# K stage in three-slot bundles, with R and convolution in K's PSUM ring: a fused convolution and channel mix on one core

## Chip, cores, metric

One core of one Trainium2 chip. The metric is device time in microseconds (us) of one execution, slowest core; here there is only one. The kernel before takes 466.56 us (median of 4 runs).

## The reference

```python
w = softmax(weight)                            # [8 heads, 7 taps]
y = causal depthwise convolution of x with w   # x: [8, 4160, 192]; 24 channels a head
y_prev = y shifted by one position
xk = mu_k * y + (1 - mu_k) * y_prev
xr = mu_r * y + (1 - mu_r) * y_prev
k = relu(xk @ w_k)                             # 192 -> 1024
v = (k * k) @ w_v                              # 1024 -> 192
out = sigmoid(xr @ w_r) * v
```

## The kernel before

A slot is one K tile: 128 of the 1024 channels of k at 512 positions of two batches (1024 columns), 8 slots a step. The batches are taken in four pairs, here called quarters, of 65 slots each. Channels are 192 = 128 + 64; the 64 rest channels of two batches lie in one tile, so their matmuls use 64-row halves of the array side by side. Two slots make a bundle, ordered so that the 64-row matmuls of both stand together:

```python
psK = tile_pool(bufs=2, PSUM)   # K tiles, two banks each
psV = tile_pool(bufs=2, PSUM)   # V, one bank each
psM = tile_pool(bufs=2, PSUM)   # convolution, transposes, R: one bank each

def k_mm(n):                    # slot n
    ps = psK.tile([P, 2, BANK], FP32, tag="k")
    first = j % 2 == 0
    go(first, True)             # even slot: 128-row matmuls, then 64-row ones; odd: the reverse
    go(not first, False)
# ... cut
at_ = n0 + ns + 2               # slot of a step's first V tile
# ... cut
for ns in bundles():            # per bundle of two slots
    for n in ns: run(early, n)  # loads of x
    for n in real: k_mm(n)
    for n in ns:
        run(act, n)             # ScalarE: convolution out of PSUM, sigmoid
        run(pe, n)              # convolution, transposes, R, V
        k_relu(n)               # ScalarE
        run(dve, n)             # VectorE: difference, mixes, v_out; SP: y_write, y_read
        k_square(n - 1)         # VectorE
```

Convolution gives y with time on partitions; K needs channels there. For the first four groups of blocks TensorE transposes y. From the fifth on y goes through memory: `y_write` stores it to `y_drams`, `y_read` fetches it with a transposing DMA into `yT`. Both are issued from the SP queue, as are all outputs.

Of the kernel before, what the change touches and what calls it, by code (L numbers as in the profile page):

```python
# [14 lines left out]
def kernel(  # L15
# [29 lines left out]
    WARM = 40  # L45
# [5 lines left out]
    psK = ctx.enter_context(tc.tile_pool(name="psK", bufs=2, space=bass.MemoryType.PSUM))  # L51
    psV = ctx.enter_context(tc.tile_pool(name="psV", bufs=2, space=bass.MemoryType.PSUM))
    psM = ctx.enter_context(tc.tile_pool(name="psM", bufs=2, space=bass.MemoryType.PSUM))
# [19 lines left out]
    for p in range(NPAIR):  # L73
        blk0 = 0
        for nb, s, on_pe in (
            ((3, 0, True), (4, 1, True), (4, 2, True), (5, 3, True), (10, 4, False), (6, 6, False), (3, 8, False))
            if p == 0
            else ((10, 0, False), (8, 2, False), (8, 4, False), (9, 6, False))
        ):
            groups.append((p, blk0, nb, steps[first_step[p] + s][3], on_pe))  # L80
            blk0 += nb
# [109 lines left out]
    def conv_mm(g, c, pool=None, tag="m"):  # L191
        nb = groups[g][2]
        if c == 0:
            ys[g] = two.tile([P, GB, 2 * D], BF16, tag="y", name="y")
        hs = chunks(g)[c]
        ps = (pool or psM).tile([P, nb, 2, G * len(hs)], FP32, tag=tag, name="ps_c")
        conv_ps[g, c] = ps
        for i, h in enumerate(hs):
            nc.tensor.matmul(  # L199
                out=ps[:, :, :, i * G : (i + 1) * G],  # L200
                lhsT=toe[:, h, :],
                rhs=xbs[g][:, :nb, :, h * G : (h + 1) * G],
                start=True,
                stop=True,
            )
# [43 lines left out]
    def tr_mm(g, j):  # L249
# [3 lines left out]
        ps = psM.tile([P, 3, 2, BLK], BF16, tag="m", name="ps_t")  # L253
# [21 lines left out]
    def diff(s):  # L275
        p, t0, L, _, _ = steps[s]
        c0 = YC + t0
        d = two.tile([P, 3, STEP], BF16, tag="diff", name="d")
# [48 lines left out]
    def k_mm(n):  # L327


        s, j = slots[n]  # L330
        p, _, L, _, _ = steps[s]
        if L == TAIL:
            return k_mm_tail(n, p)
        xk = xks[s]
        ps = psK.tile([P, 2, BANK], FP32, tag="k", name="ps_k")
        k_ps[n] = ps
        first = j % 2 == 0
        nf = STEP // L


        def go(hi, start):
            for f in range(nf):
                fs = slice((j * nf + f) * P, (j * nf + f + 1) * P)
                for i in range(2):
                    r = slice(0, P) if hi else slice(i * LO, (i + 1) * LO)
                    nc.tensor.matmul(  # L346
                        out=ps[:, i, f * L : (f + 1) * L],
                        lhsT=wk[r, 0 if hi else 1, fs],
                        rhs=xk[r, i if hi else 2, :L],
                        start=start and f == 0,  # L350
                        stop=not start and f == nf - 1,
                    )

        go(first, True)
        go(not first, False)
# [42 lines left out]
    for s, (p, t0, L, n0, ns) in enumerate(steps):  # L398
        for t in range(max(1, 2 * L // P)):
            at_ = n0 + ns + 2  # L400
            tiles.append((s, t, max(at_, tiles[-1][2] + 1) if tiles else at_))
# [3 lines left out]
    def r_mm(m):  # L405
        s, t, _ = tiles[m]
        p, _, L, _, _ = steps[s]
        q = m - t % 2
        if t % 2 == 0:
            r_ps[q] = psM.tile([P, 2, D], FP32, tag="m", name="ps_r")  # L410
        o = r_ps[q][:, t % 2, :]
        if L > TAIL:
            xr = xrs[s]
            st, c = divmod(t * P, L)
            hi, lo, wlo = xr[:, st, c : c + P], xr[:, 2, c : c + P], wr[:, 2 + st, :]
        else:
            hi, lo, wlo = tails[p % 2][:, 1, 1, :], tails[p % 2][:, 1, 0, :], wr[:, 1, :]
        nc.tensor.matmul(out=o, lhsT=hi, rhs=wr[:, 0, :], start=True, stop=False)  # L418
        nc.tensor.matmul(out=o, lhsT=lo, rhs=wlo, start=False, stop=True)  # L419

    def r_sig(m):
        ps = r_ps.pop(m)
        n = 2 if steps[tiles[m][0]][2] > TAIL else 1
        r_sb = four.tile([P, 2, D], BF16, tag="r_sb", name="r_sb")
        r_sbs[m] = r_sb
        nc.scalar.activation(out=r_sb[:, :n, :], in_=ps[:, :n, :], func=AF.Sigmoid)  # L426
# [38 lines left out]
    early, pe, act, dve = ({} for _ in range(4))  # L465
# [3 lines left out]

    for g, (p, blk0, nb, n0, on_pe) in enumerate(groups):  # L470
        if g < 2:
            continue
        nc_ = len(chunks(g))
        late = p == 0 and n0 < 30
        if not on_pe:
            per = 2 if late else 1
            c0 = n0 - 20 if late else n0 - 30
            w0, r0 = c0 + -(-nc_ // per), n0 - (11 if late else 17)
        else:
            per = 1  # L480
            c0 = n0 - 14 if n0 > 12 else 1
            r0 = c0 + nc_
        if g > 3:
            at(early, max(c0 - 14, 6 if g == 4 else 10), x_tile, g, nc.vector)
            at(early, max(c0 - 14, 6 if g == 4 else 10), load_x, g)
        for c in range(nc_):
            at(pe, c0 + c // per, conv_mm, g, c)
            at(act, c0 + c // per + 1, conv_out, g, c, nc.scalar.copy)
        if on_pe:
            for j in range((nb + 1) // 2):  # L490
                at(pe, r0 + j, tr_mm, g, j)
                at(dve, r0 + 1 + j, tr_out, g, j, nc.vector.tensor_copy)
        else:
            at(dve, w0, y_write, g)
            at(dve, r0, y_read, g)
    for s, (p, t0, L, n0, ns) in enumerate(steps):
        if s == 0:
            continue
        late = n0 < 14
        at(dve, n0 - (3 if late else 7), diff, s)  # L500
        for j, (i, part) in enumerate(((0, 0), (0, 1), (1, 0), (1, 1))):
            at(dve, n0 + ((-3, -2, -1, 0)[j] if late else j - 5), mix, s, i, part)
    for m, (s, t, vs) in enumerate(tiles):
        at(pe, vs - 2, r_mm, m)
        if t % 2 == 1 or steps[s][2] == TAIL:
            q = m - t % 2
            at(act, vs - 1, r_sig, q)
            at(dve, vs + 1, v_out, q)
        at(pe, vs, v_mm, m)

    def run(table, n):
        for fn, a in table.get(n, ()):
            fn(*a)

    def prologue():
# [23 lines left out]
        warm = psK.tile([P, BANK], FP32, tag="k", name="warm")  # L539
        for _ in range(WARM):  # L540
            nc.tensor.matmul(out=warm, lhsT=ones_t, rhs=zeros, start=True, stop=True)
# [16 lines left out]
        for c in range(n):  # L558
            conv_mm(0, c, psV if c % 2 else None, "v" if c % 2 else "m")
        for c in range(n):  # L560
            conv_out(0, c, act_ if c % 2 == 0 else dve_, act_)
        for j in range(2):
            tr_mm(0, j)
        for j in range(2):
            tr_out(0, j, dve_)
        n = len(chunks(1))
        for c in range(n):
            conv_mm(1, c, psV if c % 2 else None, "v" if c % 2 else "m")
            conv_out(1, c, act_)
        diff(0)  # L570
        for i in range(2):
            for part in range(2):
                mix(0, i, part)
        for j in range(2):
            tr_mm(1, j)
            tr_out(1, j, dve_)
# [3 lines left out]
    def bundles():  # L580

        n = 0
        while n < tiles[-1][2] + 3:
# [53 lines left out]
```

## Time and profile before

| | before |
|---|---|
| time, median | 466.56 us |
| span of the profiled run | 464.4 us |
| TensorE busy | 445.4 us, 96% |
| VectorE, ScalarE busy | 83%, 80% |
| TensorE waits from 60 to 450 us | none listed |

TensorE sets the time from 44 us on; the prediction shows those lines.

Below, a hole is a stretch in which TensorE starts no matmul.

### The profile page before, as it was taken

Reading aid. Unit: us, or ns where it says so; the run is one execution under the profiler, and the core shown is the slowest. Engines: PE = TensorE matmul, PEld = TensorE weight load, DVE = VectorE, ACT = ScalarE, POOL = GpSimd, SP = SyncE. Lnnn points to the kernel's source line nnn. Section 1 sums busy time; section 2 is a strip of 40 time slices with the busy share of each in tenths; the row PEclk is TensorE's granted clock in tenths of the full one; section 3 lists DMA queues with packets and bytes.
Section 4 is the critical chain, followed back from the end, with each engine's and each line's share of the span. In section 5 each row is a group of like instructions: output and inputs, shape, how many; then the busy total and the mean of one; then the engine's idle time right before and its main releaser. Section 6 shows DMA issues by size and latency. Waiting matters only on the chain.

```text
span 464.4 us, 10001 instructions
## 1 busy us (share of the span) xinstructions
PE 445.4 (96%) x3898; PEld 298.3 (64%) x3960; DVE 387.3 (83%) x748; ACT 371.3 (80%) x544; POOL 49.5 (11%) x71
## 2 busy tenths in 40 slices
PE   8787999999999999999999999999999999999996
PEld 3554666666876666566676666666677666666676
DVE  2887799887998889889798989878898987888873
ACT  2598878978878897888979788887978888777771
POOL 6810511000020050000002041000002000000000
PEclk9799999999999999999999999999999999999999
DMA  5993999683469599755367779938166753821223
GB/s 79 164 185 75 181 196 202 120 192 112 105 136 186 141 154 232 148 145 135 99 150 124 182 120 215 220 82 200 55 150 129 165 133 95 167 69 52 69 69 95
DMA packets 134480, 64.18 MB, mean 138 GB/s; under 512 B 85825, under 2 KB 133985, under 8 KB 134433
## 3 DMA queue, kind: packets, MB, share of 16 engines
q1 hardware_dynamic: 96097, 48.60, 41.9%
q0 software_dynamic: 38336, 14.95, 27.7%
q8 instruction: 31, 0.51, 0.5%
q14 instruction: 16, 0.13, 0.1%
HBM read 29.65 MB, written 37.25 MB: 144 GB/s over the span
## 4 chain that ended last, share of the span: by engine, by line
PE 91%; DMA 2%; DVE 2%; ACT 2%; issue 2%; POOL 0%; DVEq 0%
PE ps_k L346 39%; PE ps_v L436 37%; PE ps_r L418 5%; PE ps_r L419 5%; PE ps_c L199 4%; DMA xb<-in_x_dram 1%; ACT k_sb L375 1%; PE ps_k L363 1%; DMA w_raw<-in_weight_dram 1%; ACT y L219 1%; PE ps_t L257 1%; DMA w_scr<-w_row 1%; DVE k L394 0%; ACT y L222 0%; DVE yT L268 0%
## 5 line engine op out<-in xcount | busy, mean ns | idle before, releaser
L375 ACT ACTIVATE k_sb<-ps_k 128x1024 bf16<-128x1024 f32 x260 | 260.1, 1026 | 36.4 <-PE ps_k L346 31.6
L346 PE MATMUL ps_k<-xk,wk 64*128 64x512 bf16 (+2 forms) x994 | 205.3, 377 | 7.5 <-ACT k_sb L375 0.4
L436 PE MATMUL ps_v<-wv,k 128*128 128x192 bf16 x2048 | 210.8, 246 | 0.0
L436 PEld LDWEIGHTS <-k 128*128 128x128 bf16 x2048 | 175.3, 98 | 31.3 <-issue 1.8
L394 DVE TENSOR_TENSOR k<-k_sb 128x1024 bf16<-128x1024 bf16 x256 | 174.9, 685 | 15.0 <-ACT k_sb L375 14.3
L346 PEld LDWEIGHTS <-wk 64*128 64x128 bf16 (+1 forms) x1056 | 56.3, 96 | 109.1 <-issue 108.0
L449 DVE TENSOR_TENSOR o_sb<-ps_v,r_sb 128x384 f32<-128x384 f32 x132 | 72.4, 549 | 35.7 <-PE ps_v L436 33.8
L426 ACT ACTIVATE r_sb<-ps_r 128x384 bf16<-128x384 f32 x132 | 64.4, 488 | 39.3 <-PE ps_r L419 38.8
L418 PE MATMUL ps_r<-wr,xr 128*128 128x192 bf16 x256 | 62.9, 246 | 0.0
L419 PE MATMUL ps_r<-wr,xr 128*128 128x192 bf16 x256 | 62.9, 246 | 0.0
L219 ACT CAST y<-ps_c 120x384 bf16<-120x384 f32 (+4 forms) x96 | 45.0, 471 | 8.8 <-PE ps_c L199 8.8
L199 PE MATMUL ps_c<-xb,toe 128*128 128x384 bf16 (+6 forms) x152 | 43.5, 321 | 4.1 <-ACT y L222 1.8
L323 DVE TENSOR_TENSOR xr<-xr,yT 128x1024 bf16<-128x1024 bf16 (+1 forms) x66 | 36.2, 549 | 2.3
L323 DVE TENSOR_TENSOR xk<-xk,yT 128x1024 bf16<-128x1024 bf16 (+1 forms) x66 | 36.2, 549 | 2.3
L109 POOL DMA_DIRECT2D xb<-in_x_dram x38 | 33.5, 888 | 31.0 <-issue 17.5
L281 DVE TENSOR_TENSOR d<-yT 128x1536 bf16<-128x1536 bf16 (+2 forms) x37 | 31.8, 859 | 3.6 <-DMA yT<-y_dram 3.5
L320 DVE TENSOR_SCALAR xr<-d,mu 128x1024 bf16<-128x1024 bf16 (+1 forms) x66 | 27.9, 423 | 0.1
L108 POOL DMA_DIRECT2D xb<-in_x_dram x8 | 4.4, 552 | 221.1 <-PE ps_k L346 221.1
L320 DVE TENSOR_SCALAR xk<-d,mu 128x1024 bf16<-128x1024 bf16 (+1 forms) x66 | 26.6, 403 | 0.2
L418 PEld LDWEIGHTS <-xr 128*128 128x128 bf16 x256 | 25.0, 98 | 0.0
L419 PEld LDWEIGHTS <-xr 128*128 128x128 bf16 x256 | 25.0, 98 | 0.0
L222 ACT CAST y<-ps_c 120x384 bf16<-120x384 f32 (+9 forms) x52 | 24.0, 466 | 0.4 <-DVE yT L227 0.2
(48 smaller groups left out, 88.5 us busy)
## 6 DMA issues: line engine op xcount, KB each, us to landing
out_dram<-o_sb SPq DMA_DIRECT2D x128, 192.0 KB, 2.4
xb<-in_x_dram POOLq DMA_DIRECT2D x18, 384.0 KB, 10.4
y_dram<-y SPq DMA_DIRECT2D x6, 720.0 KB, 5.4
y_dram<-y SPq DMA_DIRECT2D x4, 900.0 KB, 6.6
xb<-in_x_dram POOLq DMA_DIRECT2D x6, 432.0 KB, 8.1
y_dram<-y SPq DMA_DIRECT2D x3, 810.0 KB, 10.4
xb<-in_x_dram POOLq DMA_DIRECT2D x2, 480.0 KB, 8.8
xb<-in_x_dram POOLq DMA_DIRECT2D x4, 192.0 KB, 6.1
```

The source lines that it names most:

```text
L199: nc.tensor.matmul(out=ps[:, :, :, i * G : (i + 1) * G], lhsT=toe[:, h, :], rhs=xbs[g][:, :nb, :, h * G : (h + 1) * G], start=True, stop=True,
L219: copy(out=yh[:, :, :, c0 : c0 + n], in_=ps[:BLK, :, :, 0:n])
L320: nc.vector.tensor_scalar(out=o, in0=d[:, sl, :L], scalar1=mu[:, i, part : part + 1], scalar2=None, op0=ALU.mult)
L323: nc.vector.tensor_tensor(out=o, in0=o, in1=yT[:, sl, c0 : c0 + L], op=ALU.add)
L346: nc.tensor.matmul(out=ps[:, i, f * L : (f + 1) * L], lhsT=wk[r, 0 if hi else 1, fs], rhs=xk[r, i if hi else 2, :L], start=start and f == ...
L375: nc.scalar.activation(out=k_sb, in_=ps.rearrange("p a b -> p (a b)"), func=AF.Relu)
L394: nc.vector.tensor_tensor(out=o, in0=i, in1=i, op=ALU.mult)
L418: nc.tensor.matmul(out=o, lhsT=hi, rhs=wr[:, 0, :], start=True, stop=False)
L419: nc.tensor.matmul(out=o, lhsT=lo, rhs=wlo, start=False, stop=True)
L426: nc.scalar.activation(out=r_sb[:, :n, :], in_=ps[:, :n, :], func=AF.Sigmoid)
L436: nc.tensor.matmul(out=o, lhsT=k2[:, f, t * P : (t + 1) * P], rhs=wv[:, f, :], start=(f == 0), stop=(f == NF - 1),)
L449: nc.vector.tensor_tensor(out=o_sb[:, :n, :], in0=v_ps.pop(m)[:, :n, :], in1=r_sbs.pop(m)[:, :n, :], op=ALU.mult)
```

## The change

The intent is fewer changes of the row tiling on TensorE (one stretch of 64-row matmuls for three slots instead of two). Three K tiles take six of the eight PSUM banks that the kernel uses, and V two, so R (four tiles at a time) and convolution (two chunks) move into the K ring (the pool whose buffers are handed out in turn), and the early schedule is written anew. Cut to its core:

```diff
-    psK = ... bufs=2        psV = ... bufs=2        psM = ... bufs=2
+    psK = ... bufs=3        psV = ... bufs=2
-        ((3,0,True),(4,1,True),(4,2,True),(5,3,True),(10,4,False),(6,6,False),(3,8,False))
+        ((3,0,True),(4,1,True),(4,2,True),(5,3,True),(10,4,False),(9,6,False))
+    def k_section(ns):
+        for n in ns[:-1]: k_mm(n, True, True)     # 128 rows
+        for n in ns[:-1]: k_mm(n, False, False)   # 64 rows
+        k_mm(ns[-1], False, True)                 # 64 rows
+        k_mm(ns[-1], True, False)                 # 128 rows
-            at_ = n0 + ns + 2
+            at_ = n0 + ns + 1
-            c0 = n0 - 20 if late else n0 - 30
-            w0, r0 = c0 + -(-nc_ // per), n0 - (11 if late else 17)
+            xs = {28: [7, 9, 11, 13], 44: [19, 22, 25, 28]}[n0] if p == 0 else range(n0 - 34, n0 - 34 + 4 * nx, 4)
+            at(dve, xs[-1] + 1, y_write, g)
+            at(dve, xs[-1] + 5, y_read, g)
+            if ns[0] < NSLOT:
+                k_section(ns)
+                for n in ns: k_relu(n)
             for n in ns:
-                run(act, n)
+                run(xt, n)      # R and convolution, matmuls and ScalarE part
                 run(pe, n)      # V (and the transposes)
```

For the first group through memory this moves `y_write` from slot 12 to 14, `y_read` from 17 to 18, and its first reader from 21 to 22. The load of x for the second quarter moves from slot 21 to 17.

More of the change, by code (lines that the diff above doesn't have):

```diff
@@ L44 @@
     YC = 16
-    WARM = 40
+    WARM = 36
     const = ctx.enter_context(tc.tile_pool(name="const", bufs=1))
@@ L50 @@
     four = ctx.enter_context(tc.tile_pool(name="four", bufs=4))
-    psK = ctx.enter_context(tc.tile_pool(name="psK", bufs=2, space=bass.MemoryType.PSUM))
+    psK = ctx.enter_context(tc.tile_pool(name="psK", bufs=3, space=bass.MemoryType.PSUM))
     psV = ctx.enter_context(tc.tile_pool(name="psV", bufs=2, space=bass.MemoryType.PSUM))
-    psM = ctx.enter_context(tc.tile_pool(name="psM", bufs=2, space=bass.MemoryType.PSUM))
     dram = ctx.enter_context(tc.tile_pool(name="dram", bufs=1, space=bass.MemoryType.DRAM))
@@ L75 @@
         for nb, s, on_pe in (
-            ((3, 0, True), (4, 1, True), (4, 2, True), (5, 3, True), (10, 4, False), (6, 6, False), (3, 8, False))
+            ((3, 0, True), (4, 1, True), (4, 2, True), (5, 3, True), (10, 4, False), (9, 6, False))
             if p == 0
-            else ((10, 0, False), (8, 2, False), (8, 4, False), (9, 6, False))
+            else ((10, 0, False), (10, 2, False), (10, 4, False), (5, 7, False))
         ):
@@ L189, in chunks, with conv_mm @@
         return [range(h, min(H, h + n)) for h in range(0, H, n)]
-    def conv_mm(g, c, pool=None, tag="m"):
+    def conv_mm(g, c):
         nb = groups[g][2]
@@ L194, in conv_mm @@
             ys[g] = two.tile([P, GB, 2 * D], BF16, tag="y", name="y")
-        hs = chunks(g)[c]
-        ps = (pool or psM).tile([P, nb, 2, G * len(hs)], FP32, tag=tag, name="ps_c")
-        conv_ps[g, c] = ps
-        for i, h in enumerate(hs):
-            nc.tensor.matmul(
-                out=ps[:, :, :, i * G : (i + 1) * G],
-                lhsT=toe[:, h, :],
-                rhs=xbs[g][:, :nb, :, h * G : (h + 1) * G],
-                start=True,
-                stop=True,
-            )
+        ps2 = psK.tile([P, 2, BANK], FP32, tag="k", name="ps_c")
+        for k, hs in enumerate(chunks(g)[c : c + 2]):
+            w = G * len(hs)
+            ps = ps2[:, k, 0 : nb * 2 * w].rearrange("p (n s c) -> p n s c", n=nb, s=2)
+            conv_ps[g, c + k] = ps
+            for i, h in enumerate(hs):
+                nc.tensor.matmul(
+                    out=ps[:, :, :, i * G : (i + 1) * G],
+                    lhsT=toe[:, h, :],
+                    rhs=xbs[g][:, :nb, :, h * G : (h + 1) * G],
+                    start=True,
+                    stop=True,
+                )
     def conv_out(g, c, copy, copy_lo=None):
@@ L252, in tr_mm @@
             new_yT(p)
-        ps = psM.tile([P, 3, 2, BLK], BF16, tag="m", name="ps_t")
+        ps = psV.tile([P, 3, 2, BLK], BF16, tag="v", name="ps_t")
         tr_ps[g, j] = ps
@@ L277, in diff @@
         c0 = YC + t0
-        d = two.tile([P, 3, STEP], BF16, tag="diff", name="d")
+        d = three.tile([P, 3, STEP], BF16, tag="diff", name="d")
         diffs[s] = d
@@ L325, with k_mm @@
     k_ps, k_sbs, k2s = {}, {}, {}
-    def k_mm(n):
+    def k_mm(n, hi, start):
         s, j = slots[n]
-        p, _, L, _, _ = steps[s]
-        if L == TAIL:
-            return k_mm_tail(n, p)
+        L = steps[s][2]
         xk = xks[s]
-        ps = psK.tile([P, 2, BANK], FP32, tag="k", name="ps_k")
-        k_ps[n] = ps
-        first = j % 2 == 0
+        if start:
+            k_ps[n] = psK.tile([P, 2, BANK], FP32, tag="k", name="ps_k")
+        ps = k_ps[n]
         nf = STEP // L
-        def go(hi, start):
-            for f in range(nf):
-                fs = slice((j * nf + f) * P, (j * nf + f + 1) * P)
-                for i in range(2):
-                    r = slice(0, P) if hi else slice(i * LO, (i + 1) * LO)
-                    nc.tensor.matmul(
-                        out=ps[:, i, f * L : (f + 1) * L],
-                        lhsT=wk[r, 0 if hi else 1, fs],
-                        rhs=xk[r, i if hi else 2, :L],
-                        start=start and f == 0,
-                        stop=not start and f == nf - 1,
-                    )
-        go(first, True)
-        go(not first, False)
+        for f in range(nf):
+            fs = slice((j * nf + f) * P, (j * nf + f + 1) * P)
+            for i in range(2):
+                r = slice(0, P) if hi else slice(i * LO, (i + 1) * LO)
+                nc.tensor.matmul(
+                    out=ps[:, i, f * L : (f + 1) * L],
+                    lhsT=wk[r, 0 if hi else 1, fs],
+                    rhs=xk[r, i if hi else 2, :L],
+                    start=start and f == 0,
+                    stop=not start and f == nf - 1,
+                )
+    def k_section(ns):
+        s, _ = slots[ns[0]]
+        if steps[s][2] == TAIL:
+            return k_mm_tail(ns[0], steps[s][0])
+        for n in ns[:-1]:
+            k_mm(n, True, True)
+        for n in ns[:-1]:
+            k_mm(n, False, False)
+        k_mm(ns[-1], False, True)
+        k_mm(ns[-1], True, False)
     def k_mm_tail(n, p):
@@ L399, with r_mm @@
         for t in range(max(1, 2 * L // P)):
-            at_ = n0 + ns + 2
+            at_ = n0 + ns + 1
             tiles.append((s, t, max(at_, tiles[-1][2] + 1) if tiles else at_))
     r_ps, r_sbs, v_ps = {}, {}, {}
-    def r_mm(m):
-        s, t, _ = tiles[m]
+    def r_mm(m0):
+        s, _, _ = tiles[m0]
         p, _, L, _, _ = steps[s]
-        q = m - t % 2
-        if t % 2 == 0:
-            r_ps[q] = psM.tile([P, 2, D], FP32, tag="m", name="ps_r")
-        o = r_ps[q][:, t % 2, :]
-        if L > TAIL:
-            xr = xrs[s]
-            st, c = divmod(t * P, L)
-            hi, lo, wlo = xr[:, st, c : c + P], xr[:, 2, c : c + P], wr[:, 2 + st, :]
-        else:
-            hi, lo, wlo = tails[p % 2][:, 1, 1, :], tails[p % 2][:, 1, 0, :], wr[:, 1, :]
-        nc.tensor.matmul(out=o, lhsT=hi, rhs=wr[:, 0, :], start=True, stop=False)
-        nc.tensor.matmul(out=o, lhsT=lo, rhs=wlo, start=False, stop=True)
@@ L421, in r_sig @@
-    def r_sig(m):
-        ps = r_ps.pop(m)
-        n = 2 if steps[tiles[m][0]][2] > TAIL else 1
-        r_sb = four.tile([P, 2, D], BF16, tag="r_sb", name="r_sb")
-        r_sbs[m] = r_sb
-        nc.scalar.activation(out=r_sb[:, :n, :], in_=ps[:, :n, :], func=AF.Sigmoid)
+        ps = psK.tile([P, 2, BANK], FP32, tag="k", name="ps_r")
+        r_ps[m0] = ps
+        for k in range(4 if L > TAIL else 1):
+            t = tiles[m0 + k][1]
+            o = ps[:, k // 2, k % 2 * D : (k % 2 + 1) * D]
+            if L > TAIL:
+                xr = xrs[s]
+                st, c = divmod(t * P, L)
+                hi, lo, wlo = xr[:, st, c : c + P], xr[:, 2, c : c + P], wr[:, 2 + st, :]
+            else:
+                hi, lo, wlo = tails[p % 2][:, 1, 1, :], tails[p % 2][:, 1, 0, :], wr[:, 1, :]
+            nc.tensor.matmul(out=o, lhsT=hi, rhs=wr[:, 0, :], start=True, stop=False)
+            nc.tensor.matmul(out=o, lhsT=lo, rhs=wlo, start=False, stop=True)
@@ new lines, in r_sig @@
+    def r_sig(m0):
+        ps = r_ps.pop(m0)
+        if steps[tiles[m0][0]][2] > TAIL:
+            r_sb = three.tile([P, 2, 2 * D], BF16, tag="r_sb", name="r_sb")
+            nc.scalar.activation(out=r_sb, in_=ps[:, :, 0 : 2 * D], func=AF.Sigmoid)
+            for k in range(2):
+                r_sbs[m0 + 2 * k] = r_sb[:, k, :].rearrange("p (t d) -> p t d", t=2)
+        else:
+            r_sb = two.tile([P, D], BF16, tag="r_tail", name="r_tail")
+            nc.scalar.activation(out=r_sb, in_=ps[:, 0, 0:D], func=AF.Sigmoid)
+            r_sbs[m0] = r_sb.unsqueeze(1)
@@ L462, in v_out, with conv, r, tr @@
                 )
-    early, pe, act, dve = ({} for _ in range(4))
+    early, xt, pe, dve = ({} for _ in range(4))
     def at(table, n, fn, *a):
         table.setdefault(n, []).append((fn, a))
+    def conv(g, c):
+        conv_mm(g, c)
+        for k in range(c, min(c + 2, len(chunks(g)))):
+            conv_out(g, k, nc.scalar.copy)
+    def r(m0):
+        r_mm(m0)
+        r_sig(m0)
+    def tr(g, j):
+        tr_mm(g, j)
+        tr_out(g, j, nc.vector.tensor_copy)
     for g, (p, blk0, nb, n0, on_pe) in enumerate(groups):
-        if g < 2:
+        nx = -(-len(chunks(g)) // 2)
+        ntr = (nb + 1) // 2
+        if g == 0:
@@ L472 @@
             continue
-        nc_ = len(chunks(g))
-        late = p == 0 and n0 < 30
-        if not on_pe:
-            per = 2 if late else 1
-            c0 = n0 - 20 if late else n0 - 30
-            w0, r0 = c0 + -(-nc_ // per), n0 - (11 if late else 17)
-        else:
-            per = 1
-            c0 = n0 - 14 if n0 > 12 else 1
-            r0 = c0 + nc_
+        if g == 1:
+            xs, trs = [], [0] * ntr
+        elif on_pe:
+            xs = [[0, 1], [4, 6]][g - 2]
+            trs = [[2, 3], [7, 8, 9]][g - 2]
+        else:
+            xs = {28: [7, 9, 11, 13], 44: [19, 22, 25, 28]}[n0] if p == 0 else range(n0 - 34, n0 - 34 + 4 * nx, 4)
+            trs = []
+            at(dve, xs[-1] + 1, y_write, g)
+            at(dve, xs[-1] + 5, y_read, g)
@@ L483 @@
         if g > 3:
-            at(early, max(c0 - 14, 6 if g == 4 else 10), x_tile, g, nc.vector)
-            at(early, max(c0 - 14, 6 if g == 4 else 10), load_x, g)
-        for c in range(nc_):
-            at(pe, c0 + c // per, conv_mm, g, c)
-            at(act, c0 + c // per + 1, conv_out, g, c, nc.scalar.copy)
-        if on_pe:
-            for j in range((nb + 1) // 2):
-                at(pe, r0 + j, tr_mm, g, j)
-                at(dve, r0 + 1 + j, tr_out, g, j, nc.vector.tensor_copy)
-        else:
-            at(dve, w0, y_write, g)
-            at(dve, r0, y_read, g)
+            at(early, max(xs[0] - 14, 5 if g == 4 else 9), x_tile, g, nc.vector)
@@ L496 @@
+            at(early, max(xs[0] - 14, 5 if g == 4 else 9), load_x, g)
+        for i, n in enumerate(xs):
+            at(xt, n, conv, g, 2 * i)
+        for j, n in enumerate(trs):
+            at(pe, n, tr, g, j)
     for s, (p, t0, L, n0, ns) in enumerate(steps):
         if s == 0:
-            continue
-        late = n0 < 14
-        at(dve, n0 - (3 if late else 7), diff, s)
-        for j, (i, part) in enumerate(((0, 0), (0, 1), (1, 0), (1, 1))):
-            at(dve, n0 + ((-3, -2, -1, 0)[j] if late else j - 5), mix, s, i, part)
+            when = (None, None, None, 1, 1)
+        elif s == 1:
+            when = (0, 0, 1, 4, 5)
+        elif s == 2:
+            when = (5, 6, 7, 9, 10)
+        elif n0 == 28:
+            when = (22, 24, 25, 27, 28)
+        else:
+            when = (n0 - 8, n0 - 6, n0 - 5, n0 - 3, n0 - 2)
@@ L503 @@
+        if when[0] is not None:
+            at(dve, when[0], diff, s)
+        for n, (i, part) in zip(when[1:], ((0, 0), (0, 1), (1, 0), (1, 1))):
+            if n is not None:
+                at(dve, n, mix, s, i, part)
     for m, (s, t, vs) in enumerate(tiles):
-        at(pe, vs - 2, r_mm, m)
+        if t % 4 == 0:
+            at(xt, 2 if s == 0 else vs - 3, r, m)
         if t % 2 == 1 or steps[s][2] == TAIL:
-            q = m - t % 2
-            at(act, vs - 1, r_sig, q)
-            at(dve, vs + 1, v_out, q)
+            at(dve, vs + 1, v_out, m - t % 2)
@@ L513, in run, with warm @@
             fn(*a)
+    def warm(n):
+        ps = psV.tile([P, BANK], FP32, tag="v", name="warm")
+        for _ in range(n):
+            nc.tensor.matmul(out=ps, lhsT=ones_t, rhs=zeros, start=True, stop=True)
     def prologue():
@@ L537, in prologue @@
         )
-        warm = psK.tile([P, BANK], FP32, tag="k", name="warm")
-        for _ in range(WARM):
-            nc.tensor.matmul(out=warm, lhsT=ones_t, rhs=zeros, start=True, stop=True)
+        warm(WARM)
         softmax()
@@ L557, in prologue @@
         n = len(chunks(0))
-        for c in range(n):
-            conv_mm(0, c, psV if c % 2 else None, "v" if c % 2 else "m")
+        for c in range(0, n, 2):
+            conv_mm(0, c)
         for c in range(n):
             conv_out(0, c, act_ if c % 2 == 0 else dve_, act_)
+        warm(2)
         for j in range(2):
@@ L565, in prologue @@
             tr_out(0, j, dve_)
+        warm(5)
         n = len(chunks(1))
-        for c in range(n):
-            conv_mm(1, c, psV if c % 2 else None, "v" if c % 2 else "m")
-            conv_out(1, c, act_)
+        for c in range(0, n, 2):
+            conv(1, c)
         diff(0)
-        for i in range(2):
-            for part in range(2):
-                mix(0, i, part)
-        for j in range(2):
-            tr_mm(1, j)
-            tr_out(1, j, dve_)
+        for part in range(2):
+            mix(0, 0, part)
+        warm(3)
         x_tile(3, nc.vector)
@@ L582, in bundles @@
         n = 0
+        for p in range(NPAIR):
+            rest = sum(st[4] for st in steps if st[0] == p and st[2] > TAIL)
+            twos = rest % 3 * -1 % 3
+            sizes = [2] * twos + [3] * ((rest - 2 * twos) // 3)
+            for w in sizes if p == 0 else sizes[::-1]:
+                yield range(n, n + w)
+                n += w
+            yield range(n, n + 1)
+            n += 1
         while n < tiles[-1][2] + 3:
-            w = 2 if n < NSLOT and steps[slots[n][0]][2] > TAIL else 1
-            yield range(n, n + w)
-            n += w
+            yield range(n, n + 1)
+            n += 1
     with tc.manual_schedule():
@@ L590 @@
         for n in range(-60, 0):
-            for table in (early, act, pe, dve):
+            for table in (early, xt, pe, dve):
                 assert n not in table, n
@@ L595 @@
                 run(early, n)
-            real = [n for n in ns if n < NSLOT]
-            for n in real:
-                k_mm(n)
+            if ns[0] < NSLOT:
+                k_section(ns)
+                for n in ns:
+                    k_relu(n)
             for n in ns:
-                run(act, n)
+                run(xt, n)
                 run(pe, n)
-                if n in real:
-                    k_relu(n)
                 run(dve, n)
```

## The prediction

> **What bounds the kernel now.** I read the page first: engine totals, then the time slices, then the groups.
>
> ```profile
> span 464.4 us, 10001 instructions
> PE 445.4 (96%) x3898; PEld 298.3 (64%) x3960; DVE 387.3 (83%) x748; ACT 371.3 (80%) x544; POOL 49.5 (11%) x71
> PE   8787999999999999999999999999999999999996
> L375 ACT ACTIVATE k_sb<-ps_k 128x1024 bf16<-128x1024 f32 x260 | 260.1, 1026 | 36.4 <-PE ps_k L346 31.6
> L394 DVE TENSOR_TENSOR k<-k_sb 128x1024 bf16<-128x1024 bf16 x256 | 174.9, 685 | 15.0 <-ACT k_sb L375 14.3
> L426 ACT ACTIVATE r_sb<-ps_r 128x384 bf16<-128x384 f32 x132 | 64.4, 488 | 39.3 <-PE ps_r L419 38.8
> ```
>
> TensorE is busy 96% of the span, and the only slices below 9 are the first four and the last. So there are two stages: a start of some 44 us with holes, and a steady stage without any. A table by windows agrees (window, length, then busy time of PE, PEld, DVE, ACT, POOL):
>
> ```profile
> 18.10:43.70 25.60, 21.47 (x166) 12.20 (x168) 20.60 (x39) 21.22 (x35) 6.60 (x9) 0.94 0.99 125
> 43.70:251.00 207.30, 204.04 (x1815) 137.95 (x1843) 182.02 (x353) 175.57 (x259) 21.61 (x28) 1.00 0.78 153
> 251.00:460.20 209.20, 205.61 (x1847) 140.64 (x1875) 177.17 (x335) 168.78 (x240) 9.57 (x12) 1.00 0.59 128
> ```
>
> In the steady stage VectorE is at 86%, ScalarE at 83%; both follow TensorE. The waits of TensorE from 60 to 450 us, listed alone, are empty. So only TensorE issue time, or the start, can make this kernel shorter. "Busy" hides one loss though, seen in the timeline of a bundle without convolution (start, length, engine, line):
>
> ```profile
> 447.25 1.67 PE L346 MATMUL ps_k<-xk,wk 128*128 128x512 bf16 x8
> 448.76 0.82 PE L436 MATMUL ps_v<-wv,k 128*128 128x192 bf16 x8
> 449.42 0.25 PE L418 MATMUL ps_r<-wr,xr 128*128 128x192 bf16 x1
> ...
> 448.21 1.94 ACT L375 ACTIVATE k_sb<-ps_k 128x1024 bf16<-128x1024 f32 x2 [0.27 <-PE ps_k L346]
> ```
>
> The K section of two slots runs from 447.25 to 448.76: 1.51 us. Its eight matmuls are four over 128 rows and two pairs of 64-row ones; the trace's start times show the two of a pair 3 to 4 ns apart. So six streams of 512 columns, 0.216 us each by the trace's starts inside a stretch, are 1.30 us. The remaining 0.21 us is the change of row tiling: start to start from the last 128-row matmul to the first 64-row one is 0.312 us, back again 0.308, and two neighbours lose 0.01 each. There are 128 such bundles: 128 x 0.206 = 26.4 us.
>
> **What the Trainium skill says.** "TensorEngine Tiling (Array Packing)", Key Properties: "Mode switching requires drain". The trace agrees: 0.096 and 0.092 us lost at the two switches. "TensorE: Matmul & The Clock Gate", Back-to-back issue gap: N/2.4 + 2.5 ns warm; the trace has 216 ns for 512 columns and 82 for 192. "PSUM — Partial Sum Buffer", Specifications: eight banks of 2 KiB per partition. The buffers fit exactly: before 2x2 (K) + 2 (V) + 2 (the rest), after 3x2 + 2; no trace shows the limit itself, but it is why R and convolution must now go through K's ring. "ScalarE: Activation LUTs", What ACT_TABLE_LOAD costs: 186 + 0.833 N ns with immediates; 1039 for N=1024 against 1026 measured, so the sigmoid over 768 elements is estimated at 0.82 us (from this trace's own 488 and 1026: 0.81).
>
> **The change, part by part.**
>
> 1. *Fewer switches.* The 256 full slots went in 128 bundles; they go in 88 now (20 of three and 2 of two in each quarter), one stretch each. 40 x 0.206 = **-8.2 us**, on the path, since TensorE is the bound.
>
> 2. *R and convolution in K's ring.* The new wait. With three tiles in the ring and a bundle that takes three (a, b, c), the next tile asked for is always a's, and it is free when ScalarE has read a. Clock from the bundle's start: four 128-row matmuls of a and b and the switch, 3 x 0.216 + 0.312 = 0.96; a's 64-row pair ends 0.39 later (durations of 376 to 387 ns), so a's relu starts at 1.40 (before: 448.21 - 447.25 = 0.96, with two matmuls fewer ahead). Two relus in a row take 1.94, so they start 0.92 apart: relu a ends at 2.42, b at 3.34, c at 4.26. A wait of TensorE on ScalarE in the start of this trace ended 0.06 after its releaser. The K section itself ends at 9 x 0.216 + 0.21 = 2.16.
>  - An R or convolution that comes straight after the section starts at 2.48 instead of 2.16: 0.32 lost. The instruction order of the changed kernel has 26 three-slot bundles after the start where just one such item stands there: 26 x 0.32 = 8.3.
>  - Four bundles have both there. Convolution is done at 2.48 + 0.40 = 2.88, R needs b's tile: 3.40. 0.32 + 0.52 = 0.84, x 4 = 3.4.
>  - Six have both after the first V tile (0.66): convolution 2.82 to 3.22, R waits to 3.40: 6 x 0.18 = 1.1.
>  - All others come late enough. In two-slot bundles at the quarters' ends the tile three back is one of the bundle before. K's own next tiles: after a bundle with both items ScalarE is done at about 4.26 + 0.81 + 1.0 = 6.1, and the next c needs its tile about 5.2 + 1.4 = 6.6.
>  Sum: **+12.8 us**, unhidden, because matmuls go in order and the V tiles that could fill the hole come behind it.
>
> 3. *ScalarE.* 128 sigmoids of 0.488 become 64 of 0.81: 62 - 52 = 10 us less, off the path. It is free again (6.1) before the next relu is due (5.2 + 1.4 = 6.6).
>
> 4. *V a slot earlier.* TensorE has the same work; no instruction is saved. The tightest case is a step whose last slot opens a bundle: its square can be ready at 2.42 + 0.69 + 0.06 = 3.17, its V tile comes at 2.16 + 1.32 = 3.48. Fits by 0.3 if VectorE isn't behind: 0.
>
> 5. *Start.* Until 43.7 us (K of slot 14) TensorE does about 18 us of matmuls from 18.1 on (counts times the intervals above) in 25.6, so at most 7 us are to be had. The first K should start near 16.3 instead of 18.1, as the second group's transposes go behind it. But VectorE then has the same chain (copies, difference, mixes, first squares) in one piece: my walk through its order has V of step 0 waiting for the fourth square until 28.5 to 29.7, and slot 13 starting at 39.9 to 42.6, against about 43.3 now. **-1 to -3.5, taken as -2.**
>
> Sum: 466.5 - 8.2 + 12.8 - 2 = 469.
>
> **The rivals.**
> (A) *The ring waits are absent or filled.* Then 466.5 - 8.2 - 3 = 455. For it: the constants of the schedule look tuned, and TensorE has had no ring wait so far in the steady stage. Against it: relu a's end (2.42) follows from measured durations and lies after the section's end; I see nothing that could reorder matmuls. I give it a quarter, mostly for errors in my positions and for a start that gains more.
> (B) *The ring waits as worked out*: 467 to 470.
> (C) *VectorE becomes the bound.* A bundle of 3 slots has 379/88 = 4.3 us of VectorE work (387 less some 8 before the main loop) in 4.9 us, and squares now come in bursts of three behind the relus. Each V tile that waits for a square would add, say, 0.3 us in a few dozen bundles: 472 to 477. Against it: VectorE keeps 0.5 us per bundle, and the psV ring lets it lag nearly two slots.
> (D) *ScalarE falls behind* in bundles with both items, so that relu a starts late and every wait of part 2 grows. By part 3 half a microsecond of slack is left; small chance, about +5.
>
> **Range and chances.** 0.75 x 469 + 0.25 x 455 = 465.5; I say 466. Faster by over 2% means under 457.2, which needs nearly all of A; slower by over 2% means over 475.8, which needs C or D on top of B. The range 456.5 to 472.5 covers B and the upper half of A.
>
> **What would show it.** Right on part 1: 88 K stretches instead of 128, and a three-slot section of 2.16 us where nothing waits. Right on part 2: waits of the first R or convolution matmul for the ScalarE relu line, near 0.3 us each, some 30 to 40 of them, 10 to 14 us in all, where before none stood after 60 us. The sigmoid group: 64 of about 0.81 us. Right on part 4: almost no waits of V for VectorE. Right on part 5: slot 13 near 40 to 42.6 us. I am wrong if TensorE has no such waits and the span is near 453 (A), or if the waits name VectorE's squares (C), or if relu a's start trails the end of its matmul (D).

## More of the kernel before

The loads of x are issued from GpSimd. `diff(s)`, a VectorE instruction, is the first reader of `yT` in step s. A line of the list of waits says who waited for whom: us in total, times, longest.

One more line of this profile matters. It is from the list of waits (who waited for whom: us in total, times, longest):

```profile
DVE d L281 <- DMA yT<-y_dram: 3.5, 1, 3.5
```

VectorE waited once for transposed y, at the first step that takes it through memory. TensorE didn't stop then.

## The result, and the profile after

489.07 us (median of 4 runs, 488.44 to 490.74) against 466.56 beside it: 4.9% slower, ratio 1.0491 (1.0461 to 1.0521). Ratios here are the mean time of one kernel's fast runs over that of the other's of the same rounds, so not quite the ratio of the medians quoted. The page of the changed kernel, the lines that answer to those of before:

```profile
span 486.7 us, 9977 instructions
PE 448.2 (92%) x3903; PEld 304.7 (63%) x3958; DVE 384.0 (79%) x748; ACT 352.1 (72%) x464; POOL 48.3 (10%) x69
PE   8778945969999999999999999999999999999996
L434 ACT ACTIVATE r_sb<-ps_r 128x768 bf16<-128x768 f32 x64 | 53.4, 834 | 4.9 <-PE ps_r L428 3.8
L283 DVE TENSOR_TENSOR d<-yT 128x1536 bf16<-128x1536 bf16 (+2 forms) x37 | 31.7, 857 | 21.6 <-DMA yT<-y_dram 21.6
```

TensorE is as busy as before and the span is 22 us longer. The slices (12.2 us each) show a 4 and a 5 from 61 to 85 us and a 6 from 97 to 109 us, where all was 9. And the difference, which waited 3.5 us for transposed y, waits 21.6. By windows (stretch, length, busy of PE, PEld, DVE, ACT, POOL, clock, DMA share, GB/s):

```profile
66.50:78.00 11.50, 0.60 (x3) 0.19 (x2) 2.96 (x5) 1.26 (x2) 0.00 (x0) 0.72 1.01 143
101.00:106.00 5.00, 0.88 (x10) 0.64 (x8) 2.02 (x4) 1.27 (x2) 0.00 (x0) 0.98 0.82 211
106.00:480.00 374.00, 365.24 (x3265) 253.50 (x3310) 319.42 (x618) 289.68 (x373) 21.95 (x28) 1.00 0.63 132
```

In the first of these windows TensorE works 0.6 of 11.5 us. The starts of its matmuls in the trace put the two holes at 11.1 and 4.3 us, and the matmuls after each run at half clock for a while (160 instead of 82 ns between V matmuls): 3.3 us more. Together 18.7.

The chain into the first hole, in the timeline of the changed kernel (start, length, engine, line; SPq is the SP queue):

```profile
48.61 0.41 SPq L236 DMA_DIRECT2D y_dram<-y  x1
50.93 1.00 POOL L108 DMA_DIRECT2D xb<-in_x_dram  x1
52.46 2.91 POOL L108 DMA_DIRECT2D xb<-in_x_dram  x3
56.34 11.69 SPq L244 DMA_TRANSPOSE yT<-y_dram  x1
64.55 2.32 PE L344 MATMUL ps_k<-xk,wk 128*128 128x512 bf16 x11
75.03 0.96 DVE L283 TENSOR_TENSOR d<-yT 128x1536 bf16<-128x1536 bf16 x1 [15.80 <-DMA yT<-y_dram]
76.69 2.09 ACT L382 ACTIVATE k_sb<-ps_k 128x1024 bf16<-128x1024 f32 x2 [12.36 <-DVE k L401]
77.77 0.88 PE L201 MATMUL ps_c<-xb,toe 128*128 128x432 bf16 x2 [10.90 <-ACT k_sb L382]
```

Read it from the end: convolution waits for the relu to leave a K tile (the ring), the relu waits for the square to free `k_sb`, the square stands behind the difference on VectorE, and the difference waits 15.8 us for the read issued at 56.34. Same steps in the kernel before:

```profile
42.48 0.41 SPq L234 DMA_DIRECT2D y_dram<-y  x1
48.47 0.55 POOL L108 DMA_DIRECT2D xb<-in_x_dram  x1 [20.65 <-PE ps_k L346]
49.51 4.98 SPq L242 DMA_TRANSPOSE yT<-y_dram  x1
54.47 0.56 POOL L103 DMA_DIRECT2D xb<-in_x_dram  x1 [3.46 <-PE ps_r L419]
```

Time from issue to landing of the reads from 40 to 112 us, before and then after (min, median, max of four and of two reads; the first read is the longest in both):

```profile
DMA to landing us min/median/max: 3.3/6.8/9.3
```

```profile
DMA to landing us min/median/max: 6.4/12.6/18.7
```

The first read is issued 6.8 us later and takes 18.7 instead of 9.3 us. It is issued 0.02 us after the write of y has landed (7.7 us after the write's issue), so it follows the write and not its own slot. Beside it run two groups of x loads (the POOL lines). In the kernel before, a small group (some 0.3 MB) was issued at 48.5 us, just ahead of the read; the loads of the second quarter were issued from 54.5 us on, and most of their packets moved after 58 us, when the read had landed. The Trainium skill says in "DMA: Bandwidth & Descriptors", Issuing engines are not separate DMA queues, that DMAs of the scalar, sync or gpsimd engine "will ultimately run on the same 16 DMA engines and interleave with each other". The packets of the traces, told apart by size, agree: from 62 to 70 us the x loads moved 190 to 215 KB in each 2 us and the read 125 to 145. Before, at 52 to 56 us, the read moved 360 to 385, beside 55 to 100 of x; in run e1 below, with no x load beside it, up to 550.

The second hole, at 101 us, has the loads beside the write of y rather than the read:

```profile
87.86 0.36 SPq L236 DMA_DIRECT2D y_dram<-y  x1
97.51 4.47 SPq L244 DMA_TRANSPOSE yT<-y_dram  x1
103.98 0.96 DVE L283 TENSOR_TENSOR d<-yT 128x1536 bf16<-128x1536 bf16 x1 [5.77 <-DMA yT<-y_dram]
```

x loads were issued at 86.7 us; the write took 9.6 us to land (6.2 in run e5, without them), the read was issued as it landed, and itself took only 6.4 us.

The waits that I did predict stand in the steady stage. TensorE's timeline, one section with R behind it and one with V:

```profile
400.38 2.32 PE L344 MATMUL ps_k<-xk,wk 128*128 128x512 bf16 x11
402.84 0.24 PE L427 MATMUL ps_r<-wr,xr 128*128 128x192 bf16 x1
...
410.84 2.32 PE L344 MATMUL ps_k<-xk,wk 128*128 128x512 bf16 x12
412.99 0.25 PE L450 MATMUL ps_v<-wv,k 128*128 128x192 bf16 x1
```

```profile
401.77 2.85 ACT L382 ACTIVATE k_sb<-ps_k 128x1024 bf16<-128x1024 f32 x3 [1.28 <-PE ps_k L344]
```

From section start to V 2.15 us, to R 2.46. Over the run the medians are 2.155 where V follows (46 sections) and 2.466 where R or convolution does (32): 0.311 us each. "Idle" in the list of waits hardly shows them, because the modelled ends of the matmuls reach into the gap; the starts do.

### The profile page after: what moved, and what is told of

The parts are those of the page before. It is cut to its first block, busy times and chain, and to the rows that moved or that the text cites. A ratio compares the mean times of both kernels' runs of the same rounds, so it can differ in the third digit from the quotient of the medians.

```text
span 486.7 us, 9977 instructions
## 1 busy us (share of the span) xinstructions
PE 448.2 (92%) x3903; PEld 304.7 (63%) x3958; DVE 384.0 (79%) x748; ACT 352.1 (72%) x464; POOL 48.3 (10%) x69
## 4 chain that ended last, share of the span: by engine, by line
PE 71%; DMA 11%; ACT 8%; DVE 5%; issue 2%; POOL 1%; DVEq 0%; ACTq 0%
PE ps_v L450 30%; PE ps_k L344 28%; ACT k_sb L382 7%; DMA yT<-y_dram 5%; PE ps_r L427 4%; PE ps_r L428 4%; DMA y_dram<-y 4%; PE ps_c L201 3%; DVE k L401 2%; DMA xb<-in_x_dram 2%; PE ps_k L370 1%; ACT y L221 1%; ACT y L224 1%; DMA w_raw<-in_weight_dram 1%; DVE xk L325 1%
## 5 line engine op out<-in xcount | busy, mean ns | idle before, releaser
L382 ACT ACTIVATE k_sb<-ps_k 128x1024 bf16<-128x1024 f32 x260 | 248.4, 1024 | 105.7 <-PE ps_k L344 82.3
L450 PE MATMUL ps_v<-wv,k 128*128 128x192 bf16 x2048 | 197.0, 247 | 5.2 <-DVE k L401 4.5
L344 PE MATMUL ps_k<-xk,wk 64*128 64x512 bf16 (+2 forms) x1002 | 193.8, 373 | 5.5 <-issue 3.3
L401 DVE TENSOR_TENSOR k<-k_sb 128x1024 bf16<-128x1024 bf16 x256 | 172.2, 682 | 2.1 <-ACT k_sb L382 2.1
L344 PEld LDWEIGHTS <-wk 128*128 128x128 bf16 (+1 forms) x1056 | 61.7, 96 | 102.7 <-issue 74.0
L434 ACT ACTIVATE r_sb<-ps_r 128x768 bf16<-128x768 f32 x64 | 53.4, 834 | 4.9 <-PE ps_r L428 3.8
L427 PE MATMUL ps_r<-wr,xr 128*128 128x192 bf16 x256 | 48.5, 249 | 6.2 <-DVE xr L325 2.4
L283 DVE TENSOR_TENSOR d<-yT 128x1536 bf16<-128x1536 bf16 (+2 forms) x37 | 31.7, 857 | 21.6 <-DMA yT<-y_dram 21.6
L428 PE MATMUL ps_r<-wr,xr 128*128 128x192 bf16 x256 | 48.5, 249 | 0.3 <-DVE xr L325 0.3
L221 ACT CAST y<-ps_c 120x480 bf16<-120x480 f32 (+5 forms) x85 | 40.1, 538 | 11.8 <-PE ps_c L201 11.6
L201 PE MATMUL ps_c<-xb,toe 128*128 128x480 bf16 (+4 forms) x144 | 32.6, 327 | 14.1 <-ACT k_sb L382 10.9
L428 PEld LDWEIGHTS <-xr 128*128 128x128 bf16 x256 | 25.3, 99 | 11.4 <-issue 10.5
L201 PEld LDWEIGHTS <-toe 128*128 128x128 bf16 x144 | 13.2, 98 | 21.8 <-issue 18.3
```

The source lines that it names most:

```text
L201: nc.tensor.matmul(out=ps[:, :, :, i * G : (i + 1) * G], lhsT=toe[:, h, :], rhs=xbs[g][:, :nb, :, h * G : (h + 1) * G], start=True, stop=True,
L221: copy(out=yh[:, :, :, c0 : c0 + n], in_=ps[:BLK, :, :, 0:n])
L344: nc.tensor.matmul(out=ps[:, i, f * L : (f + 1) * L], lhsT=wk[r, 0 if hi else 1, fs], rhs=xk[r, i if hi else 2, :L], start=start and f == ...
L382: nc.scalar.activation(out=k_sb, in_=ps.rearrange("p a b -> p (a b)"), func=AF.Relu)
L401: nc.vector.tensor_tensor(out=o, in0=i, in1=i, op=ALU.mult)
L427: nc.tensor.matmul(out=o, lhsT=hi, rhs=wr[:, 0, :], start=True, stop=False)
```

## Experiments

Each was run in 3 rounds beside the kernel before; all results were correct. Medians, and the ratio to the kernel before of the same chip. The diffs are shortened.

### e1: the x load later

```diff
-  at(early, max(xs[0] - 14, 5 if g == 4 else 9), x_tile / load_x, g)
+  e = 25 if g == 6 else max(xs[0] - 14, 5 if g == 4 else 9)
+  at(early, e, x_tile / load_x, g)
```

> The changed kernel with one edit: the load of x for the first group of the second quarter (and with it the loads queued behind it) is issued at slot 25, behind the difference of slot 28's step, instead of slot 17. Theory COLLISION (the transposing read of y lands 18.7 us after its issue, against 9.3 before, because two groups of x are loaded at the same time): the read lands in 9 to 11 us, the difference waits some 6 instead of 15.8 us, TensorE idles 1 to 3 instead of 11 us there, and the time falls by 9 to 12 us to 477-480. Theory LATE (the read is simply issued 6.8 us later than before with the same deadline): landing stays above 15 us, time stays at 487-490. The second wait near 101 us may stay or grow by a few us.

482.14 us, 1.0345. The SP queue and VectorE of this run:

```profile
54.76 3.82 SPq L244 DMA_TRANSPOSE yT<-y_dram  x1
...
84.53 9.10 SPq L244 DMA_TRANSPOSE yT<-y_dram  x1
```

```profile
60.65 0.96 DVE L283 TENSOR_TENSOR d<-yT 128x1536 bf16<-128x1536 bf16 x1 [2.02 <-DMA yT<-y_dram]
97.25 0.96 DVE L283 TENSOR_TENSOR d<-yT 128x1536 bf16<-128x1536 bf16 x1 [12.38 <-DMA yT<-y_dram]
```

The first read lands in 5.9 us, the difference waits 2.0 instead of 15.8, and the first hole is gone. The loads now run beside the second write and the second read of y: 10.0 and 12.7 us to landing, a wait of 12.4, a hole of 10.9 instead of 4.3. The gain of 7 us is under the expected 9 to 12 for that reason. LATE is out: the first read was issued only 1.6 us sooner than in the changed kernel.

### e2: convolution and y earlier

```diff
-  {28: [7, 9, 11, 13], 44: [19, 22, 25, 28]}
+  {28: [5, 7, 9, 11],  44: [14, 16, 18, 20]}
```

> The changed kernel with one edit: the convolution of the two groups behind the first DMA transposes is moved to slots 5,7,9,11 and 14,16,18,20 (from 7,9,11,13 and 19,22,25,28), so that y is written and read back earlier. If the whole miss of 20 us over the prediction's sum is the two waits for the transposed y and the cold clock behind them, both waits vanish and the time is 467 to 473. If the slow 18.7 us of the read is in the read itself, a wait of some us stays and the time is 474 to 480. If the loss is elsewhere: above 485.

478.62 us, 1.0291 (runs from 478.09 to 483.77, the profile in the longest): a miss of 467 to 473. It lies in the range set for a read that is slow in itself (474 to 480), but e1 rules that out: there the read landed in 5.9 us. The earlier convolution found its x not landed (2.0 us), crowded the start, and y was written at 49.2 us, no sooner than in the changed kernel (48.6). The reads took 16.6 and 12.7 us with x loads beside them, and the difference still waited 7.9. An earlier slot doesn't help a transfer that is slow because of its company.

### b2: the load earlier, in the kernel before

```diff
+  e = 17 if g == 7 else max(c0 - 14, 6 if g == 4 else 10)   # was slot 21 for g == 7
```

> The kernel BEFORE with one edit: the load of x for the first group of the second quarter is issued at slot 17 instead of 21, so that it and the one queued behind it run beside the first transposing read (49.5 to 58.8 us). Nothing of the change is in it. COLLISION: the read lands in 14 us or more instead of 9.3, the difference waits 8 us or more instead of 3.5, and the time grows by 3 to 12 us, 469-478. If x loads beside the read do not matter: 465-467.

470.32 us, 1.0081 (1.0063 to 1.0099). This kernel has nothing of the change but the load's slot. Its list of waits and the landing of its reads:

```profile
DVE d L281 <- DMA yT<-y_dram: 8.3, 1, 8.3
```

```profile
DMA to landing us min/median/max: 3.2/5.8/13.8
```

The read takes 13.8 instead of 9.3 us, the wait grows from 3.5 to 8.3, and a TensorE hole of 3.5 us appears at 62.6 us. COLLISION holds without the rest of the change, though the 13.8 us and the 3.5 us of time are at the low end of what it expected.

### e5: x loads away from both reads

```diff
+  elif g > 6 and blk0 > 0:
+      eng.memset(xb[0:32, 0, 0, 0:2], 0.0)    # holds a load to its slot
-  at(early, max(xs[0] - 14, 5 if g == 4 else 9), ...)
+  e = {6: 10, 7: 37}.get(g, max(xs[0] - 14, 5 if g == 4 else 9))
+  at(early, e, ...)
```

> The changed kernel with only the times of the x loads altered: the load for the first group of the second quarter is issued at slot 10 (before y of the first DMA group is written) instead of 17; the next one at slot 37, held there by a tiny memset on VectorE; later ones are held to their slot in the same way. So neither transposing read of y in the first quarter has x loads beside it. COLLISION: both reads land in 5 to 8 us, TensorE's two holes of 11.1 and 4.3 us and the cold clock behind them go, and the time is 468 to 472: the sum of the prediction (469), with the ring waits still in it (32 sections of 2.47 instead of 2.16 us). LATE (deadline alone): a hole of 5 us or more stays, 475 or more.

472.31 us, 1.0121 (1.0105 to 1.0136), at the upper edge of the expected range. Its VectorE waits:

```profile
DVE d L285 <- DMA yT<-y_dram: 8.6, 5, 2.6
```

The largest is 2.6 us and one TensorE hole of 1.1 us is left after the start. Sections followed by R or convolution still last 2.466 us. So 17 of the 22.5 us of the loss go with the times of the x loads alone; what remains over the kernel before is near the sum of the prediction (469).

For the first read, the runs make all four cases. Read early, big loads elsewhere (before): VectorE waits 3.5 us, no hole. Early with the loads beside it (b2): a hole of 3.5 us. Late without them (e1, e5): no hole. Late with them (the changed kernel): 11.1 us. The loads make the hole; the later issue alone costs nothing, but it takes away what would have hidden part of it.

### e3 and e7: V ahead of R and convolution

```diff
+  run(pe, n)
   run(xt, n)
-  run(pe, n)
```

e3 is the changed kernel with this edit, e7 is e5 with it.

> The changed kernel with V (and the transposes) ahead of R and convolution inside each slot. Theory RING (R or convolution straight after a K section waits 0.31 us for ScalarE to leave the first K tile; 30-odd times): the waits go except some 0.15 us in four bundles, time falls by 9 to 13 us to 476-480. Rival MOVED: R and convolution come later, so their tiles are read later and the next K section waits for them instead; then the time is 485 to 490 and K's matmuls show the waits. The two waits for transposed y stay.

> e5_paced with V and transposes ahead of R and convolution in each slot as well. If the ring waits (12 us in the profile of the changed kernel) are then the only loss left against the sum of matmuls: 457 to 462, faster than the kernel before by 1 to 2%. If V first only brings VectorE or output waits in (three such holes of 1.4 to 3.3 us stood in e3_v_first after 180 us): 464 to 470.

e3: 485.67 us, 1.0432. e7: 469.05, 1.0046. All three-slot sections but two fall to 2.155 us; of 12 us of ring waits 0.7 to 0.9 stay. The time of e3 lies in the range of MOVED, but K does not wait instead, so MOVED is out. e3 missed the 476 to 480 of RING, and e7 fell in its second range, 464 to 470, because new holes came: of 1.4 to 3.3 us after 180 us in e3, and six after 120 us in e7. V first also shortens the start: slot 13 begins at 41.1 us in e3 and 40.8 in e7, against 43.2 in the changed kernel and 43.8 in e5, so not all of the gain is ring waits. VectorE and the SP queue of e3 at the first of them:

```profile
185.10 0.69 DVE L401 TENSOR_TENSOR k<-k_sb 128x1024 bf16<-128x1024 bf16 x1
192.40 0.56 DVE L463 TENSOR_TENSOR o_sb<-ps_v,r_sb 128x384 f32<-128x384 f32 x1 [6.61 <-DMA out_dram<-o_sb]
```

```profile
174.81 7.20 SPq L244 DMA_TRANSPOSE yT<-y_dram  x1
182.10 13.80 SPq L468 DMA_DIRECT2D out_dram<-o_sb  x6
```

The issue of one transposing read holds the SP queue 7.2 us; the outputs stand behind it, all four `o_sb` buffers are in use, and VectorE waits 6.6 us for one.

### e9 and e10: more output buffers

```diff
+  eight = ctx.enter_context(tc.tile_pool(name="eight", bufs=8))
-  o_sb = four.tile(...)
+  o_sb = eight.tile(...)
```

e9 is e7 with this; e10 also has `44: [16, 19, 22, 25]`.

> e7_paced_v with eight buffers of o_sb instead of four. In e7_paced_v VectorE waited 11.0 us for output transfers, which stand in the SP queue behind transposing reads whose issue takes 7 to 11 us; TensorE's six holes after 120 us (about 8 us in all) follow. If the four buffers make the VectorE wait: those holes go and the time is 459 to 463, faster than the kernel before by about 1%. If the outputs are late whatever the buffers: 466 to 470.

> e9_osb8 with the convolution of the second DMA group three slots earlier (16,19,22,25), so that its y is read back some 5 us sooner and the hole of 2.0 us near 84 us goes. Expected 457 to 461, 1 to 3 us under e9_osb8; if the earlier items crowd the start, no gain.

e9: 462.42 us, 0.9896 (0.9879 to 0.9913), 1% faster than the kernel before. e10: 461.89, 0.9891 (0.9854 to 0.9927), not told apart from e9 and just over the expected 457 to 461: the hole near 84 us went, one of 3.6 us came at 171 us. In e9 VectorE no longer waits for output transfers; its page:

```profile
span 460.3 us, 10044 instructions
PE 444.7 (97%) x3958; PEld 302.7 (66%) x3958; DVE 381.8 (83%) x754; ACT 355.7 (77%) x464; POOL 47.9 (10%) x69
PE   8789999899999999999999999999999999999996
```

Holes of 1.1 to 1.6 us (three, 3.9 us) are left. Each follows a wait of VectorE for transposed y (3.1 to 3.8 us): two directly, the one at 126 us while VectorE, busy since 119.5 us, works off what had piled up.

### e4 and e12: bundles of two

```diff
-  twos = rest % 3 * -1 % 3
+  twos = rest // 2
```

e4 is the changed kernel with this edit, e12 is e9 with it.

> The changed kernel with all bundles of two slots, so 128 stretches of 64-row matmuls again. By the sum of the prediction: 40 more switches cost 8.2 us, but with two K tiles a bundle the next item of the ring takes a tile of the bundle before, so the waits of 0.31 us (about 12 us in all) go: net 3 to 5 us faster than the changed kernel, 484-487. If switches cost nothing in time: 476-479. If the ring waits do not go: 495-498. The two waits for transposed y stay.

> e9_osb8 (462.4 us) with all bundles of two slots: 128 stretches of 64-row matmuls instead of 88, without ring waits and without the holes of the changed kernel. Part 1 of the prediction puts 40 stretches at 8.2 us: 469 to 472. If the shorter bundles hide it (fewer waits on VectorE): 463 to 467. In e4_twos the same edit did not move the time, as the ring waits went at the same time and the start was 2.9 us later.

e4: 488.96 us, 1.0488, the same as the changed kernel and over the expected 484 to 487. Sections last 1.507 us (median), whatever follows, so the ring waits are all but gone (12.0 to 1.9 us); 40 more stretches cost 8.4, and slot 16 starts 1.2 us later (not the 2.9 that the text for e12 gives the start). The two effects cancel, to within 2 us that I did not trace. e12: 467.39, 1.0003, so bundles of three are worth 5.0 us in the clean layout. It missed both ranges, lying between them: by intervals the 40 stretches cost their 8 us, but the short bundles also have 4.4 us fewer holes and small waits.

### e8 and e11: V a slot later

```diff
-  at_ = n0 + ns + 1        r at vs - 3
+  at_ = n0 + ns + 2        r at vs - 4
```

e8 is the changed kernel, e11 is e5, each with this edit.

> The changed kernel with V (and v_out) a slot later again as in the kernel before, R left in its slot. The prediction put the value of the earlier V at 0: 487-491, the same as the changed kernel. If V a slot earlier makes TensorE wait for VectorE's squares: faster, by the sum of those waits, below 485. If the earlier V is a gain at the end: slower by under 1 us.

> e5_paced (no x loads beside the early reads) with V a slot later, as in the kernel before. e8_v_lag2 was 8 us slower than the changed kernel, where the prediction had 0. If V's slot matters only as slack while VectorE waits for transposed y (TensorE then has one V tile more to do before it stops): here, with those waits small, 471 to 475, within 2 us of e5_paced. If V a slot earlier is worth something by itself: 477 to 482.

e8: 497.16 us, 1.0648, outside all that was expected. e11: 477.35, 1.0205. So V a slot earlier is worth 8.1 and 5.0 us, where the prediction had 0. In e8 the four holes add up to 20.2 us against 15.4 in the changed kernel, in e11 two holes of 3.7 and 1.4 us come up at 179 and 293 us; all but 1 to 3 us of the difference lies in such holes. In each of these V waits for VectorE's output product (`v_out`), which is held up; at 179 us in e11 the difference waited 7.3 us for y, at 198 us in e8 6.8. In e5 and the changed kernel there was no wait for y at that place, so the expectation that the worth would vanish without the early waits was wrong. By the traces this is the collision again: these reads took 19.3 us (e11) and 18.7 (e8) to land, with a big x load issued just before them; in e5 and the changed kernel the read was issued just before that load, and took 11.0 and 11.4 us. That this order decides it is argued; no run changes it alone.

## Why the prediction was wrong, point by point

Predicted 466 (456.5 to 472.5); measured 489.07.

- **Part 1, switches: right.** 88 sections, 2.155 us for three slots (2.16 predicted), 0.211 us of it for the two switches. The -8.2 us are there in the intervals; in the time they are worth 5.0 once nothing else is in the way (e12 against e9).
- **Part 2, ring waits: right.** 0.311 us each (0.32 predicted), 11.9 us in all (12.8 predicted); V first takes them away. As named in advance, R or convolution waits for ScalarE's relu.
- **Part 3: right.** 64 sigmoids of 0.834 us (0.81 predicted; the other estimate there, 186 + 0.833 x 768 ns, comes to 0.83 and not 0.82), and ScalarE is never the last to be ready in the steady stage but for these waits.
- **Part 4, V earlier, 0 us: wrong in size.** It gained 5 to 8 us, against waits of VectorE for transposed y that I had not counted (e8, e11).
- **Part 5, the start: the step that failed.** "-1 to -3.5, taken as -2". Slot 13 started at 43.2 us against the 43.3 that I gave for before: no gain up to there. (The 43.3 was itself misread: in the trace of before, the first matmul of slot 13 starts at 42.4 us.) The forecast start of 39.9 to 42.6 us came only with V first: 40.5 to 41.1 us in e3, e7 and e9. And I ended the start at slot 13 and walked VectorE's order only for arithmetic. The first difference on y from memory comes at slot 22. The diff moved its write two slots and its read one slot later and the load of x four slots earlier; I read none of these as transfers that share the DMA engines. That cost 18.7 us: two holes (11.1 and 4.3) and the half clock behind them (3.3).
- **The rivals.** None was a transfer. (C) put a VectorE bound at 472 to 477 from its busy time; VectorE did hold TensorE up, but idle, waiting for a DMA. The 3.5 us wait for y in the list of the kernel before was the hint.

With the measured terms the sum closes: 466.5 - 8.2 + 11.9 + 0 (start) + 18.7 = 488.9. V's earlier slot has no term of its own: its worth lies in holes that would be longer without it (20.2 us in e8). Shown by experiment: the collision (e1 and e5 remove it, b2 makes it in the other kernel), the ring waits (e3, e7), the output buffers (e9). Not settled: whether the order of read and load alone makes the late reads of e8 and e11, and what bundles of two cost at the start.

## What to carry to other kernels

When a change moves slots, list the transfers too: when each is issued, what else is in flight then, and when its first reader comes; a small wait on a transfer in the old profile is a transfer with no slack. A load that is paced only by a free buffer runs whenever that comes free; hold it to a slot if it must not run beside a transfer whose reader is waiting. Before two users share a ring, work out when the oldest tile comes free, and put work that needs no new tile first.

## What the Trainium skill lacked or had wrong

- "TensorEngine Tiling (Array Packing)", Key Properties, says that a mode switch drains TensorE but gives no figure: here 0.096 us into 64-row tiles and 0.092 back, 0.21 for a stretch with its neighbours.
- "DMA: Bandwidth & Descriptors", Rules for kernel authors, says that a transpose next to ordinary DMAs "needs nothing". That is said of correctness, and all results here were correct; of time it says nothing, and there the company matters: the same read landed in 18.7 us beside x loads and in 5.9 without them.
- No page says that the issue of a DMA transpose holds its queue longer when other loads run beside it: 3.8 us without and 11.7 us with x loads, and outputs issued from the same queue waited (VectorE idle 6.6 us for a buffer).
